# Turning the down products of the last four rows of a fused attention and MoE kernel

## The chip, the cores and the metric

The kernel runs on one core of a Trainium2 chip. Its time is the device time of one execution in microseconds (us). Three runs of the kernel before gave 603.53, 605.04 and 608.01 us, median 605.04.

A core has TensorE (PE, with its weight loads shown apart as PEld), VectorE (DVE), ScalarE (ACT), GpSimd (POOL) and SyncE (SP). Each runs its own list of instructions in order and waits on semaphores. DMAs are issued here by SP (all loads) and by ACT (the stores).

## The reference, cut to what matters

A linear attention with a decaying state, then a gated feed-forward layer, all in fp32:

```
for t in range(768):                                   # B=4, H=8, D=48
    cur = einsum('bhd,bhe->bhde', u * k_t, v_t)
    y[:, :, t] = einsum('bhd,bhde->bhe', r_t, state + cur)
    state = w_t[..., None] * state + einsum('bhd,bhe->bhde', k_t, v_t)
x = y as [3072 tokens, 384]
out = (sigmoid(x @ w_gate) * (x @ w_val)) @ w_out      # 384 -> 1536 -> 384
```

## The kernel before, in words

The sequence of 768 is cut into 6 rows (n = 0 to 5) of 128 positions. A row holds 4 batches of 128 tokens, so 512 tokens. For every row and batch (q = 4n + batch) an attention chunk is computed on all engines. Its result is transposed on PE (px) into x, split in a high and a low part.

The feed-forward layer then goes through 12 blocks f of the hidden size. A step (n, f) does 9 matmuls for the gate (pg), 9 for the value (pu), and on ACT and DVE the sigmoid (sg), the product with pu (sg again), its high part (hh, ACT) and its low part (hl, DVE). The down products (po) add the block's share to the row's outputs. Each product of fp32 values is done as three matmuls of parts: low by high, high by low, high by high.

In gate and value the weights (128x128) are loaded into the array and x streams past, 512 tokens wide. In the down products before, the hidden block of one batch (hl or hh, 128x128) is loaded, and 384 weight columns stream past: 4 batches by 3 parts are 12 matmuls of 384 columns. Each batch has its own PSUM bank, po0 to po3. After f = 11 ACT copies the four banks to SBUF (tile o, two buffers) and issues a DMA of 192 KB for each (L515, L517).

Rows 0 and 1 are placed by a planner, which interleaves them with the loads, the weights' unpacking and the attention. Rows 2 to 5 follow in an order written out by hand ("late"). Each step of a row runs, in this order: the gate, one part of the attention chunk of the next row, the value, another part, the down products **of the step before**, a third part. Three steps hold one attention chunk. I call them A (pk behind the gate, the score products pa behind the value), B (pa behind the gate, px behind the value) and C (nothing of the attention on PE). Row 5 has no next row, so all its steps are like C. The attention uses two PSUM banks in turn (att).

At the end a flag, computed in row 5's first step, is read by every engine (L651). A branch then jumps over `general`, a slow version for extreme inputs that is not executed here, to the end of the program, where SP waits for all DMAs and engines.

Of the kernel before, what the change touches and what calls it, by code (L numbers as in the profile page):

```python
# [9 lines left out]
F32 = mybir.dt.float32  # L10
F32R = mybir.dt.float32r
BF16 = mybir.dt.bfloat16
# [7 lines left out]
B, H, S, D = 4, 8, 768, 48  # L20
DM, DFF = 384, 1536
P = 128
C = 128
NC_ = S // C
NG = B * NC_
# [4 lines left out]
NFF = DFF // P  # L30
NKT = DM // P
# [13 lines left out]
def general(ctx: ExitStack, tc: tile.TileContext, dec, tok, wts, u, out, whi, wlo, ident):  # L45


    nc = tc.nc
    pool = ctx.enter_context(tc.tile_pool(name="general", bufs=1))
    bank = ctx.enter_context(tc.tile_pool(name="banks", bufs=1, space=PSUM))  # L50
    rows = ctx.enter_context(tc.tile_pool(name="rows", bufs=1, space=bass.MemoryType.DRAM)).tile([B, S, DM], F32, name="rows")

    def tiles(name, shape, dtype=F32):
        return pool.tile(shape, dtype, name=name)

    raw, t, full, square = tiles("raw", [P, HW], mybir.dt.int64), tiles("t", [P, HW], I32), tiles("full", [P, HW]), tiles("square", [P, HW])
    for f in range(NFF):
        for half in range(2):
            cols = slice(half * HW, (half + 1) * HW)
# [19 lines left out]
    vb, y = tiles("vb", [L, B, NP, D]), tiles("yb", [2, B, NP, D])  # L79
# [11 lines left out]
    for c in range(NC_):  # L91
        for b in range(B):
            nc.sync.dma_start(d[:, b], dec[b * NC_ + c])
        with tc.For_i(0, C) as i:
            def at(first, step):
                return d[:, :, first:first + NP * step].rearrange("a b (p c) -> a b p c", c=step)[:, :, :, bass.ds(i, 1)].broadcast_to(shape)
            for o in range(2):
                for b in range(B):
                    nc.sync.dma_start(vb[64 * o:64 * o + D, b], values[c, 2, o, bass.ds(i, 1), b].partition_broadcast(D))
            nc.vector.tensor_tensor(out=kv, in0=vb, in1=at(WW, C), op=ALU.mult)  # L100
            nc.vector.tensor_tensor(out=mix, in0=kv, in1=ub, op=ALU.mult)
            nc.vector.tensor_tensor(out=mix, in0=mix, in1=state, op=ALU.add)
            nc.vector.tensor_tensor(out=mix, in0=mix, in1=at(WW + NP * C, C), op=ALU.mult)
            nc.vector.tensor_tensor(out=state, in0=state, in1=at(1, W1), op=ALU.mult)
            nc.vector.tensor_tensor(out=state, in0=state, in1=kv, op=ALU.add)
            for j in range(2):
                nc.tensor.matmul(py[j][:2, :DM], lhsT=heads, rhs=mix[:, 2 * j:2 * j + 2], start=True, stop=True)
                nc.scalar.copy(y[:, 2 * j:2 * j + 2], py[j][:2, :DM].rearrange("a (b p e) -> a b p e", b=2, e=D))
            for b in range(B):
                for o in range(2):  # L110
                    nc.sync.dma_start(
                        rows[b, bass.ds(c * C + i, 1)].rearrange("t (p o e) -> o t p e", o=2, e=D)[o], y[o:o + 1, b])

    x, px = tiles("x", [P, DM]), bank.tile([P, 512], F32, name="px")
    xhi, xlo = tiles("xh", [P, NKT, C], F32R), tiles("xl", [P, NKT, C], F32R)
    gate, h, hh, hl = tiles("gate", [P, C]), tiles("h", [P, C]), tiles("hh", [P, C], F32R), tiles("hl", [P, C], F32R)
    pg, pu, po = (bank.tile([P, 512], F32, name=n) for n in ("pg", "pu", "po"))
    flat = rows.rearrange("b s e -> (b s) e")
    with tc.For_i(0, NG) as g:
        nc.sync.dma_start(x, flat[bass.ds(g * C, C)])  # L120
        for k in range(NKT):
            nc.tensor.transpose(out=px[:, k * C:(k + 1) * C], in_=x[:, k * P:(k + 1) * P], identity=ident)
        px3 = px[:, :DM].rearrange("a (k c) -> a k c", c=C)
        nc.scalar.copy(xhi, px3)
        nc.vector.tensor_tensor(out=xlo, in0=px3, in1=xhi.bitcast(F32), op=ALU.subtract)
        for f in range(NFF):
            for s, acc in enumerate((pg, pu)):
                for k in range(NKT):
                    cols = slice(s * DM + k * P, s * DM + (k + 1) * P)
                    for j, (w, a) in enumerate(((wlo, xhi), (whi, xlo), (whi, xhi))):  # L130
                        nc.tensor.matmul(acc[:, :C], lhsT=w[f][:, cols], rhs=a[:, k], start=k == 0 and j == 0, stop=k == NKT - 1 and j == 2)
            nc.scalar.activation(gate, pg[:, :C], AF.Sigmoid)
            nc.vector.tensor_tensor(out=h, in0=pu[:, :C], in1=gate, op=ALU.mult)
            nc.scalar.copy(hh, h)
            nc.vector.tensor_tensor(out=hl, in0=h, in1=hh.bitcast(F32), op=ALU.subtract)
            for j, (a, w) in enumerate(((hl, whi), (hh, wlo), (hh, whi))):
                nc.tensor.matmul(po[:, :DM], lhsT=a, rhs=w[f][:, 2 * DM:], start=f == 0 and j == 0, stop=f == NFF - 1 and j == 2)
        nc.scalar.copy(x, po[:, :DM])
        nc.sync.dma_start(out[bass.ds(g * C, C)], x)


class Plan:
# [49 lines left out]
def tile_kernel(ctx: ExitStack, tc: tile.TileContext, dec: bass.AP, tok: bass.AP, wts: bass.AP, u: bass.AP, out: bass.AP):  # L192
    nc = tc.nc
# [3 lines left out]
    p1 = own.enter_context(tc.tile_pool(name="p1", bufs=1))  # L197
    p2 = own.enter_context(tc.tile_pool(name="p2", bufs=2))
    ps1 = own.enter_context(tc.tile_pool(name="ps1", bufs=1, space=PSUM))
    att2 = own.enter_context(tc.tile_pool(name="att2", bufs=2, space=PSUM))  # L200
    early = tc.tile_pool(name="early", bufs=4)
    stage = early.__enter__()

    def att_bank(name):
        return att2.tile([P, 512], F32, tag="att", name=name)

    ident = const.tile([P, P], F32, name="ident")
# [8 lines left out]
    for s in range(2):  # L216
        part = after[s * HC:(s + 1) * HC]
        nc.gpsimd.affine_select(
            out=part, in_=part, pattern=[[1, HC]], compare_op=ALU.is_gt, fill=0.0, base=0, channel_multiplier=-1,
# [14 lines left out]
    raws, fulls, whi, wlo = {}, {}, [None] * NFF, [None] * NFF  # L234
# [5 lines left out]
    def word(f, i, dtype=I32):  # L240
        return raws[f].bitcast(dtype).rearrange("a (c w) -> a c w", w=2)[:, :, i]

    def w_guard(f):
        sq = p1.tile([P, 3 * DM], F32, tag="sq", name=f"sq{f}")
        nc.scalar.activation(sq, word(f, 1, F32), AF.Square, accum_out=acc_s[:, f:f + 1])
        nc.scalar.activation(sq, sq, AF.Relu, bias=1.0, scale=-1.0 / TINY ** 2, accum_out=acc_t[:, f:f + 1])

# [22 lines left out]
    pin, tk, eg, bon, kT, att, ready, mid, bank, x = {}, {}, {}, {}, {}, {}, {}, {}, {}, {}  # L270

    def place(q):
        return q % B * NC_ + q // B
# [204 lines left out]
    po, hid = {}, {}  # L478

    def gate(n, f, i0, i1):  # L480
        hid["g", n, f, i0] = up(0, "pg", n, f, i0, i1)
# [5 lines left out]
    def value(n, f, i0, i1):  # L487
        hid["u", n, f, i0] = up(1, "pu", n, f, i0, i1)
# [13 lines left out]
    def down(n, f, i0, i1):  # L502
        hh, hl = hid["hi", n, f, i0], hid["lo", n, f, i0]
        for i in range(i0, i1):
            if f == 0:
                po[n, i] = ps1.tile([P, 512], F32, tag=f"po{i}", name=f"po{n}_{i}")
            c = slice((i - i0) * C, (i - i0 + 1) * C)
            for j, (h, w) in enumerate(((hl, whi), (hh, wlo), (hh, whi))):
                nc.tensor.matmul(  # L509
                    po[n, i][:, :DM], lhsT=h[:, c], rhs=w[f][:, 2 * DM:],  # L510
                    start=f == 0 and j == 0, stop=f == NFF - 1 and j == 2,
                )
            if f == NFF - 1:
                o = p2.tile([P, DM], F32, tag="o", name=f"o{n}_{i}")
                nc.scalar.copy(o, po[n, i][:, :DM])  # L515
                g = place(n * B + i)
                nc.scalar.dma_start(out[g * C:(g + 1) * C, :], o)  # L517

    def check_bounds():
        nc.vector.tensor_scalar(out=fine[:L, 0], in0=acc_d, scalar1=2.0 ** 90, scalar2=None, op0=ALU.is_le)  # L520
# [18 lines left out]
    for q in range(3 * B + 2):  # L539
        k = rank.get(f"c{q}", 99)  # L540
# [28 lines left out]
        first = q % B == 0  # L569
# [4 lines left out]
    for f in range(NFF):  # L574
        k = rank[f"w{f}"]
# [7 lines left out]
    for g, (n, i0, i1) in enumerate(GROUPS):  # L583
        m = i1 - i0
        for f in range(NFF):
            a, name = (n, f, i0, i1), f"{g}_{f}"
            k = 100 + f + LAGS[g]
# [40 lines left out]
    last = []  # L628
    nothing = [[lambda: None] * 3] * 3
    for n in range(2, NC_):  # L630
        for j in range(B):
            trio = steps((n + 1) * B + j) if n + 1 < NC_ else nothing
            for i in range(3):
                a = (n, 3 * j + i, 0, B)
                gate(*a)
                sigmoid(*a)
                trio[i][0]()
                value(*a)
                hidden(*a)
                hidden_hi(*a)  # L640
                hidden_lo(*a)
                trio[i][1]()
                if last:
                    down(*last.pop())
                trio[i][2]()
                last.append(a)
                if n == NC_ - 1 and j == 0 and i == 0:
                    check_bounds()
    down(*last.pop())
    own.close()  # L650
    with tc.If(nc.values_load(flag[:1, :1]) != 0):  # L651
        general(tc, dec, tok, wts, u, out, whi, wlo, ident)
# [31 lines left out]
```

## Time and profile before

| | us |
|---|---|
| runs, median (lowest to highest) | 605.04 (603.53 to 608.01) |
| profiled execution, its own time | 603.9 |
| its span | 602.2 |
| PE busy | 558.7 (93%) |
| PE weight loads busy | 498.4 (83%) |
| DVE busy | 332.6 (55%) |
| ACT busy | 201.6 (33%) |

The span is what the trace covers; 1.7 us of the execution lie around it. Times in the rows count from the span's start. Matmuls overlap in the trace, so the pace of a train of matmuls is read from the starts of two neighbouring groups and not from the durations.

### The profile page before, as it was taken

The page shows a single profiled execution, that of the slowest core. Times are in us where ns is not written, and L with a number is a line of the kernel's source. Part 1 is how long each engine was busy: PE and PEld are TensorE (multiplying, and loading weights), DVE is VectorE, ACT ScalarE, POOL GpSimd, SP SyncE. Part 2 cuts the span into 40 slices and gives each one's busy share as a digit, 9 for nine tenths or more (in the row PEclk, how much of TensorE's full clock was granted, in tenths as well). Part 3 has the DMA queues.
Part 4 walks back from the last instruction along what each step waited for, and adds up shares of the span by engine and source line. Part 5 has one row for each costly group of instructions (what it writes and reads, how often), then busy time and mean ns, then how long its engine had stood idle before and what let it go on. Part 6 is the DMA issues. An engine that isn't in the chain of part 4 may idle for free. (4 is left out here: it accounts for less than half of the span.)

```text
span 602.2 us, 14593 instructions
## 1 busy us (share of the span) xinstructions
PE 558.7 (93%) x6474; PEld 498.4 (83%) x6474; DVE 332.6 (55%) x570; ACT 201.6 (33%) x402; POOL 96.7 (16%) x86
## 2 busy tenths in 40 slices
PE   4475899999999999899999999999999999999994
PEld 3365799999999999788888888888888888888883
DVE  4989879989685653254554554554454453221220
ACT  3648683444333322312222322222321221222212
POOL 3352111102120502002201211211211210000000
PEclk9999699999999999999999999999999999999997
DMA  8788920033233130122033033022033000100001
GB/s 250 250 327 290 347 95 1 1 87 83 72 121 126 50 125 3 53 86 86 3 87 87 28 112 86 2 86 87 35 106 87 1 1 2 54 1 0 1 1 57
DMA packets 12055, 50.85 MB, mean 84 GB/s; under 512 B 1376, under 2 KB 4576, under 8 KB 10448
## 3 DMA queue, kind: packets, MB, share of 16 engines
q1 hardware_dynamic: 8528, 45.11, 23.4%
q10 hardware_dynamic: 3456, 4.72, 2.2%
q8 instruction: 53, 0.87, 0.6%
q14 instruction: 18, 0.15, 0.1%
HBM read 45.11 MB, written 4.72 MB: 83 GB/s over the span
## 5 line engine op out<-in xcount | busy, mean ns | idle before, releaser
L474 PE MATMUL pg<-x,w 128*128 128x256 f32 (+1 forms) x864 | 171.6, 344 | 2.1 <-DVE w L267 2.1
L474 PE MATMUL pu<-x,w 128*128 128x256 f32 (+1 forms) x864 | 170.5, 342 | 0.0
L474 PEld LDWEIGHTS pg<-x,w 128*128 128x128 f32 x864 | 138.3, 193 | 17.8 <-DVE w L267 2.2
L474 PEld LDWEIGHTS pu<-x,w 128*128 128x128 f32 x864 | 136.2, 191 | 17.3
L509 PE MATMUL po<-w,hh 128*128 128x384 f32 x576 | 147.7, 337 | 0.0
L492 DVE TENSOR_TENSOR sg<-pu,sg 128x256 f32<-128x256 f32 (+1 forms) x96 | 53.4, 557 | 149.9 <-PE pu L474 148.9
L509 PE MATMUL po<-w,hl 128*128 128x384 f32 x288 | 101.2, 351 | 7.1 <-DVE hl L500 7.0
L496 ACT CAST hh<-sg 128x256 fp32r<-128x256 f32 (+1 forms) x96 | 49.2, 512 | 170.0 <-DVE sg L492 169.6
L509 PEld LDWEIGHTS po<-w,hh 128*128 128x128 f32 x576 | 105.0, 189 | 0.9
L485 ACT ACTIVATE sg<-pg 128x256 f32<-128x256 f32 (+1 forms) x96 | 46.9, 488 | 141.7 <-PE pg L474 140.1
L314 POOL TENSOR_TENSOR bon<-tok,a 128x384 f32<-128x384 f32 x24 | 35.0, 1457 | 282.7 <-DVE a L310 282.7
L500 DVE TENSOR_TENSOR hl<-sg,hh 128x256 fp32r<-128x256 f32 (+1 forms) x96 | 55.7, 580 | 39.0 <-ACT hh L496 39.0
L509 PEld LDWEIGHTS po<-w,hl 128*128 128x128 f32 x288 | 54.3, 189 | 10.4 <-DVE hl L500 8.4
L303 POOL TENSOR_TENSOR bon<-tok,ub 128x384 f32<-128x384 f32 x24 | 32.6, 1358 | 113.4 <-DMA tok<-tok 61.1
L448 DVE TENSOR_TENSOR bon<-pa,bon 128x192 f32<-128x192 f32 x48 | 15.6, 353 | 49.3 <-PE pa L441 49.2
L348 ACT ACTIVATE junk<-eg 112x1032 bf16<-112x1032 f32 x24 | 25.6, 1066 | 30.7 <-DVE eg L338 30.6
L321 DVE TENSOR_TENSOR_SCAN eg<-pin,ends 112x516 f32<-112x516 f32 x24 | 30.0, 1251 | 4.9 <-DMA pin<-dec 4.9
L338 DVE TENSOR_TENSOR_SCAN eg<-pin,heads 112x516 f32<-112x516 f32 x24 | 30.5, 1270 | 0.0
L353 PE MATMUL pk<-ident,pin 112*128 112x112 f32 x96 | 14.7, 278 | 14.1 <-DVE pin L327 10.2
L306 POOL TENSOR_TENSOR bon<-bon,tok 128x384 f32<-128x384 f32 x24 | 27.3, 1136 | 1.7
L441 PE MATMUL pa<-tok,at 64*32 64x48 f32 x1536 | 23.8, 213 | 2.3 <-DVE at L402 2.3
L353 PEld LDWEIGHTS pk<-ident,pin 112*128 112x128 f32 x96 | 11.5, 150 | 17.1 <-issue 9.0
(62 smaller groups left out, 433.8 us busy)
## 6 DMA issues: line engine op xcount, KB each, us to landing
pin<-dec SPq DMA_DIRECT2D x23, 675.5 KB, 5.8
tok<-tok SPq DMA_DIRECT2D x24, 576.0 KB, 5.8
wraw<-wts SPq DMA_DIRECT2D x12, 1152.0 KB, 12.3
y<-o ACTq DMA_DIRECT2D x24, 192.0 KB, 1.9
pin<-dec SPq DMA_DIRECT2D x1, 448.0 KB, 4.3
pin<-dec SPq DMA_DIRECT2D x1, 227.5 KB, 2.9
ub<-u SPq DMA_DIRECT2D x1, 192.0 KB, 6.7
```

What stands on the lines that cost most here:

```text
L303: nc.gpsimd.tensor_tensor(out=bon[q], in0=tk[q][:, 0:DM], in1=ub, op=ALU.mult)
L306: nc.gpsimd.tensor_tensor(out=bon[q], in0=bon[q], in1=tk[q][:, DM:2 * DM], op=ALU.mult)
L314: nc.gpsimd.tensor_tensor(out=by_head(bon[q]), in0=by_head(tk[q][:, 2 * DM:]), in1=a0, op=ALU.mult)
L321: nc.vector.tensor_tensor_scan(out=e[:, 516:0:-1], data0=t[:, 516:0:-1], data1=ends[:, 516:0:-1], initial=0.0, op0=ALU.mult, op1=ALU.add,)
L338: nc.vector.tensor_tensor_scan(out=e[:, WW:WW + 516], data0=t[:, 0:516], data1=heads[:, 0:516], initial=0.0, op0=ALU.mult, op1=ALU.add,)
L353: nc.tensor.transpose(out=t[:, p * L:(p + 1) * L], in_=kk(q)[:, p], identity=ident[:L, :L])
L474: nc.tensor.matmul(t, lhsT=w[f][:, cols], rhs=x[n][:, a, k, i0 * C:i1 * C], start=k == 0 and j == 0, stop=k == NKT - 1 and j == 2)
L485: nc.scalar.activation(sg, hid["g", n, f, i0], AF.Sigmoid)
L492: nc.vector.tensor_tensor(out=sg, in0=hid["u", n, f, i0], in1=sg, op=ALU.mult)
L496: nc.scalar.copy(hh, hid["s", n, f, i0])
L500: nc.vector.tensor_tensor(out=hl, in0=hid["s", n, f, i0], in1=hid["hi", n, f, i0].bitcast(F32), op=ALU.subtract)
L509: nc.tensor.matmul(po[n, i][:, :DM], lhsT=h[:, c], rhs=w[f][:, 2 * DM:], start=f == 0 and j == 0, stop=f == NFF - 1 and j == 2,)
```

## The change

The diff, without the comments and without the fallback `general`, whose layout follows the new output and whose loop over the 24 chunks is written out:

```
+    late = False
+    turns = []
     def att_bank(name):
+        turns.append(name)
+        if late and len(turns) % 3 == 0:
+            return ps1.tile([P, 512], F32, tag="po3", name=name)
         return att2.tile([P, 512], F32, tag="att", name=name)
...
     def w_guard(f):
-        sq = p1.tile([P, 3 * DM], F32, tag="sq", name=f"sq{f}")
+        sq = p1.tile([P, 3 * DM], BF16, tag="sq", name=f"sq{f}")
...
                 o = p2.tile([P, DM], F32, tag="o", name=f"o{n}_{i}")
                 nc.scalar.copy(o, po[n, i][:, :DM])
-                g = place(n * B + i)
-                nc.scalar.dma_start(out[g * C:(g + 1) * C, :], o)
+                nc.scalar.dma_start(out[n].rearrange("(b c e) -> b c e", b=B, c=C)[i], o)
+
+    def down_turned(n, f, i0, i1):
+        hh, hl = hid["hi", n, f, i0], hid["lo", n, f, i0]
+        for k in range(NKT):
+            if f == 0:
+                po[n, k] = ps1.tile([P, 512], F32, tag=f"po{k}", name=f"po{n}_{k}")
+            cols = slice(2 * DM + k * P, 2 * DM + (k + 1) * P)
+            for j, (h, w) in enumerate(((hl, whi), (hh, wlo), (hh, whi))):
+                nc.tensor.matmul(po[n, k], lhsT=w[f][:, cols], rhs=h, start=f == 0 and j == 0, stop=f == NFF - 1 and j == 2)
+            if f == NFF - 1:
+                o = p1.tile([P, B * C], F32, tag=f"ot{k}", name=f"o{n}_{k}")
+                y = po[n, k]
+                by_vector = n == NC_ - 1 and k == 1
+                if by_vector:
+                    nc.vector.tensor_copy(out=o, in_=y)
+                else:
+                    nc.scalar.copy(o, y)
+                to = out[n].rearrange("(k p t) -> k p t", p=P, t=B * C)[k]
+                (nc.sync if by_vector else nc.scalar).dma_start(to, o)
...
     stage = own.enter_context(tc.tile_pool(name="late", bufs=2))
+    late = True
...
-                    down(*last.pop())
+                    down_turned(*last.pop())
...
-    down(*last.pop())
+    down_turned(*last.pop())
```

In rows 2 to 5 the down weights (three blocks k of 128 output columns) are loaded and the 512 tokens of hl or hh stream past: 3 blocks by 3 parts are 9 matmuls of 512 columns. The outputs stand transposed in three banks, po0 to po2; the host turns them back. A row leaves as three DMAs of 256 KB in pieces of 2048 bytes instead of four of 192 KB in pieces of 1536. Each of the three has its own SBUF tile. In the last row the middle block is copied by DVE and issued by SP. The fourth bank, po3, becomes a third one for the attention in the late rows. The squares that the weights' guard computes are kept in bf16.

On PE the last two rounds of down products (f = 10 and f = 11 of row 5) read before (po, hl and hh as above, w the weights, the number behind a name its buffer):

```order
L474 MATMUL pu_0_11_6669<-x_5459,w_1682 128x512 x9
L509 MATMUL po_0_6290<-w_1558,hl_0_10_6643 128x384
L509 MATMUL po_0_6290<-w_1558,hh_0_10_6641 128x384 x2
...
L509 MATMUL po_3_6302<-w_1558,hh_0_10_6641 128x384 x2
L509 MATMUL po_0_6290<-w_1682,hl_0_11_6682 128x384
L509 MATMUL po_0_6290<-w_1682,hh_0_11_6680 128x384 x2
...
L509 MATMUL po_3_6302<-w_1682,hh_0_11_6680 128x384 x2
```

and now:

```order
L494 MATMUL pu_0_11_6518<-x_5379,w_1682 128x512 x9
L546 MATMUL po_0_6170<-hl_0_10_6495,w_1558 128x512
L546 MATMUL po_0_6170<-hh_0_10_6493,w_1558 128x512 x2
...
L546 MATMUL po_2_6178<-hh_0_10_6493,w_1558 128x512 x2
L546 MATMUL po_0_6170<-hl_0_11_6531,w_1682 128x512
L546 MATMUL po_0_6170<-hh_0_11_6529,w_1682 128x512 x2
...
L546 MATMUL po_2_6178<-hh_0_11_6529,w_1682 128x512 x2
```

Nothing else of PE's order has moved, here or in the earlier rows; only the down groups of rows 2 to 5 have other matmuls.

On ACT, the end of the program before:

```order
L515 COPY o_0_6699<-po_0_6290 128x384
L517 DMA y<-o_0_6699 128x384
L515 COPY o_1_6705<-po_1_6294 128x384
L517 DMA y<-o_1_6705 128x384
L515 COPY o_2_6711<-po_2_6298 128x384
L517 DMA y<-o_2_6711 128x384
L515 COPY o_3_6717<-po_3_6302 128x384
L517 DMA y<-o_3_6717 128x384
L651 TENSOR_LOAD flag
L651 COMPARE_AND_BRANCH
```

and now:

```order
L554 COPY o_0_6545<-po_0_6170 128x512
L556 DMA y<-o_0_6545 128x512
L554 COPY o_2_6557<-po_2_6178 128x512
L556 DMA y<-o_2_6557 128x512
L691 TENSOR_LOAD flag
L691 COMPARE_AND_BRANCH
```

Two of four copies and DMAs are gone from ACT's end; DVE has one more copy there. On SP, where the last load was followed by the flag and the branch:

```order
L281 DMA pin_5697<-dec 112x1544
L286 DMA tok_5699<-tok 128x1152
L651 TENSOR_LOAD flag
L651 COMPARE_AND_BRANCH
```

there stands now:

```order
L301 DMA pin_5607<-dec 112x1544
L306 DMA tok_5609<-tok 128x1152
L556 DMA y<-o_1_6551 128x512
L691 TENSOR_LOAD flag
L691 COMPARE_AND_BRANCH
```

SP's flag and branch now stand behind a DMA that waits for the last row's middle block.

## Rows read from the trace of the kernel before

**Rows 1.** The page: busy us (share of the span) and instructions, granted clock by slices.
```profile
PE 558.7 (93%) x6474; PEld 498.4 (83%) x6474; DVE 332.6 (55%) x570; ACT 201.6 (33%) x402; POOL 96.7 (16%) x86
...
PEclk9999699999999999999999999999999999999997
```

**Rows 2.** Busy time by stretches: us from-to, length, engines, granted clock, DMA share, GB/s.
```profile
0.00:90.00 90.00, 59.78 (x977) 53.61 (x978) 72.74 (x104) 57.13 (x101) 24.85 (x31) 0.94 0.76 261
...
285.00:390.00 105.00, 105.00 (x1164) 90.46 (x1163) 55.10 (x97) 28.38 (x57) 20.68 (x15) 1.00 0.20 60
```

**Rows 3.** Timeline of PE, a C step: start, us, line, operation, count.
```profile
287.57 2.20 PE L474 MATMUL pu<-x,w 128*128 128x512 f32 x9
289.61 0.33 PE L509 MATMUL po<-w,hl 128*128 128x384 f32 x1
...
291.19 0.33 PE L509 MATMUL po<-w,hl 128*128 128x384 f32 x1
...
291.71 0.39 PE L474 MATMUL pg<-x,w 128*128 128x512 f32 x1
```

**Rows 4.** Timeline of PE in row 1, where trains are 256 columns wide.
```profile
238.28 1.24 PE L474 MATMUL pg<-x,w 128*128 128x256 f32 x9
239.36 1.24 PE L474 MATMUL pu<-x,w 128*128 128x256 f32 x9
```

**Rows 5.** Timeline of PE, an A step and a B step of row 2.
```profile
269.35 2.25 PE L474 MATMUL pg<-x,w 128*128 128x512 f32 x9
271.44 0.55 PE L353 MATMUL pk<-ident,pin 112*128 112x112 f32 x4
271.75 2.33 PE L474 MATMUL pu<-x,w 128*128 128x512 f32 x9
274.01 0.69 PE L370 MATMUL pa<-pin 48*64 48x64 f32 x32
...
275.08 0.44 PE L509 MATMUL po<-w,hl 128*128 128x384 f32 x1
...
277.27 2.25 PE L474 MATMUL pg<-x,w 128*128 128x512 f32 x9
279.44 0.26 PE L380 MATMUL pa<-ready,pin 48*64 48x48 f32 x2
...
280.87 2.34 PE L474 MATMUL pu<-x,w 128*128 128x512 f32 x9
283.05 0.49 PE L453 MATMUL px<-ident,bon 128*128 128x128 f32 x3
283.30 0.42 PE L509 MATMUL po<-w,hl 128*128 128x384 f32 x1
...
285.49 0.39 PE L474 MATMUL pg<-x,w 128*128 128x512 f32 x1
```

**Rows 6.** Timeline of PE and ACT at the end of the program.
```profile
591.51 0.44 PE L509 MATMUL po<-w,hl 128*128 128x384 f32 x1
591.79 0.51 PE L509 MATMUL po<-w,hh 128*128 128x384 f32 x2
...
593.35 0.51 PE L509 MATMUL po<-w,hh 128*128 128x384 f32 x2
...
592.34 0.48 ACT L515 COPY o<-po 128x384 f32<-128x384 f32 x1 [1.61 <-PE po L509]
592.85 0.34 ACTq L517 DMA_DIRECT2D y<-o  x1
...
593.79 1.03 ACTq L517 DMA_DIRECT2D y<-o  x1
595.92 0.48 ACT L515 COPY o<-po 128x384 f32<-128x384 f32 x1 [2.16 <-SPq L651]
...
597.38 0.64 ACTq L517 DMA_DIRECT2D y<-o  x1
```

**Rows 7.** The flag and branch, L651, by engine: durations ns min/median/max, first and last start.
```profile
L651 SPq EVENT_SEMAPHORE  x8: 17/17/17, 526.4 to 599.7; - x8
L651 SPq TENSOR_LOAD <-flag x1: 572/572/572, 522.9 to 522.9; - x1
...
L651 SPq COMPARE_BRANCH  x1: 45/45/45, 523.6 to 523.6; - x1
...
L651 PEldq COMPARE_BRANCH  x1: 3757/3757/3757, 592.2 to 592.2; - x1
...
L651 ACTq TENSOR_LOAD <-flag x1: 485/485/485, 598.1 to 598.1; - x1
L651 ACTq COMPARE_BRANCH  x1: 54/54/54, 598.6 to 598.6; - x1
L651 ACTq EVENT_SEMAPHORE  x1: 17/17/17, 601.3 to 601.3; - x1
```

**Rows 8.** The program's last line, L680, on SP, the same columns.
```profile
L680 SPq EVENT_SEMAPHORE  x10: 17/28/1137, 599.8 to 602.1; - x10
```

**Rows 9.** Groups by shape: busy us, mean ns of one, then idle before, releaser.
```profile
L485 ACT ACTIVATE sg<-pg 128x512 f32<-128x512 f32 x48 | 28.5, 593 | 104.2 <-PE pg L474 103.4 <-PE pa L380 0.8
L492 DVE TENSOR_TENSOR sg<-pu,sg 128x512 f32<-128x512 f32 x48 | 33.2, 692 | 119.9 <-PE pu L474 119.9
L348 ACT ACTIVATE junk<-eg 112x1032 bf16<-112x1032 f32 x24 | 25.6, 1066 | 30.7 <-DVE eg L338 30.6
L246 ACT ACTIVATE sq<-sq 128x1152 f32<-128x1152 f32 x12 | 14.0, 1166 | 0.4
```

**Rows 10.** All waits from 262 to 590: who waited for whom, us, times, longest.
```profile
ACT o L515 <- DMA y<-o: 4.5, 6, 1.0
...
PE total L527 <- DVE count L525: 0.7, 1, 0.7
```

**Rows 11.** DMA issues from 585: KB each, median us to landing.
```profile
y<-o ACTq DMA_DIRECT2D x4, 192.0 KB, 2.6
```

**Rows 12.** Timeline at the start of the late rows, 249 to 252.
```profile
249.56 0.48 ACT L515 COPY o<-po 128x384 f32<-128x384 f32 x1 [0.47 <-PE po L509]
...
251.03 0.55 PE L353 MATMUL pk<-ident,pin 112*128 112x112 f32 x4
```

More of the change, by code (lines that the diff above doesn't have):

```diff
@@ L50, in general @@
     bank = ctx.enter_context(tc.tile_pool(name="banks", bufs=1, space=PSUM))
-    rows = ctx.enter_context(tc.tile_pool(name="rows", bufs=1, space=bass.MemoryType.DRAM)).tile([B, S, DM], F32, name="rows")
+    rows = ctx.enter_context(tc.tile_pool(name="rows", bufs=1, space=bass.MemoryType.DRAM)).tile([NC_, B, C, DM], F32, name="rows")
     def tiles(name, shape, dtype=F32):
@@ L111, in general @@
                     nc.sync.dma_start(
-                        rows[b, bass.ds(c * C + i, 1)].rearrange("t (p o e) -> o t p e", o=2, e=D)[o], y[o:o + 1, b])
+                        rows[c, b, bass.ds(i, 1)].rearrange("t (p o e) -> o t p e", o=2, e=D)[o], y[o:o + 1, b])
     x, px = tiles("x", [P, DM]), bank.tile([P, 512], F32, name="px")
@@ L117, in general, with feed @@
     pg, pu, po = (bank.tile([P, 512], F32, name=n) for n in ("pg", "pu", "po"))
-    flat = rows.rearrange("b s e -> (b s) e")
-    with tc.For_i(0, NG) as g:
-        nc.sync.dma_start(x, flat[bass.ds(g * C, C)])
+    def feed(n, b, turned):
+        nc.sync.dma_start(x, rows[n, b])
         for k in range(NKT):
@@ L135, in general @@
             nc.vector.tensor_tensor(out=hl, in0=h, in1=hh.bitcast(F32), op=ALU.subtract)
-            for j, (a, w) in enumerate(((hl, whi), (hh, wlo), (hh, whi))):
-                nc.tensor.matmul(po[:, :DM], lhsT=a, rhs=w[f][:, 2 * DM:], start=f == 0 and j == 0, stop=f == NFF - 1 and j == 2)
-        nc.scalar.copy(x, po[:, :DM])
-        nc.sync.dma_start(out[bass.ds(g * C, C)], x)
+            for k in range(NKT if turned else 1):
+                cols = slice(2 * DM + k * P, 2 * DM + (k + 1) * P)
+                for j, (a, w) in enumerate(((hl, whi), (hh, wlo), (hh, whi))):
+                    first, done = f == 0 and j == 0 and k == 0, f == NFF - 1 and j == 2
+                    if turned:
+                        nc.tensor.matmul(po[:, k * C:(k + 1) * C], lhsT=w[f][:, cols], rhs=a, start=first, stop=done, skip_group_check=True)
+                    else:
+                        nc.tensor.matmul(po[:, :DM], lhsT=a, rhs=w[f][:, 2 * DM:], start=first, stop=done)
+        nc.scalar.copy(x, po[:, :DM])
+        if turned:
+            to = out[n].rearrange("(k p b c) -> b p k c", p=P, b=B, c=C)[b]
+            nc.sync.dma_start(to, x.rearrange("p (k c) -> p k c", c=C))
+        else:
+            nc.sync.dma_start(out[n].rearrange("(b c e) -> b c e", b=B, c=C)[b], x)
+    for n in range(NC_):
+        for b in range(B):
+            feed(n, b, n >= 2)
 class Plan:
@@ L515, in down @@
                 nc.scalar.copy(o, po[n, i][:, :DM])
-                g = place(n * B + i)
-                nc.scalar.dma_start(out[g * C:(g + 1) * C, :], o)
+                nc.scalar.dma_start(out[n].rearrange("(b c e) -> b c e", b=B, c=C)[i], o)
[4 more added lines that the diff above has]
+                po[n, k] = ps1.tile([P, 512], F32, tag=f"po{k}", name=f"po{n}_{k}")
+            cols = slice(2 * DM + k * P, 2 * DM + (k + 1) * P)
+            for j, (h, w) in enumerate(((hl, whi), (hh, wlo), (hh, whi))):
[6 more added lines that the diff above has]
+                    nc.vector.tensor_copy(out=o, in_=y)
+                else:
+                    nc.scalar.copy(o, y)
+                to = out[n].rearrange("(k p t) -> k p t", p=P, t=B * C)[k]
+                (nc.sync if by_vector else nc.scalar).dma_start(to, o)
     def check_bounds():
@@ L678 @@
     args = [nc.dram_tensor(n, a.shape, mybir.dt.from_np(a.dtype), kind="ExternalInput").ap() for n, a in arrays.items()]
-    args.append(nc.dram_tensor("y", (B * S, DM), F32, kind="ExternalOutput").ap())
+    args.append(nc.dram_tensor("y", (NC_, B * C * DM), F32, kind="ExternalOutput").ap())
     with tile.TileContext(nc) as tc:
@@ L682 @@
     r = run_bass_kernel_spmd(nc, [arrays], core_ids=[0])
-    return r.results[0]["y"]
+    y = r.results[0]["y"]
+    y = np.concatenate([y[:2].reshape(-1, B * C, DM), y[2:].reshape(-1, DM, B * C).transpose(0, 2, 1)])
+    return np.ascontiguousarray(y.reshape(NC_, B, C, DM).transpose(1, 0, 2, 3).reshape(B * S, DM))
```

## The prediction, made blind

> **What bounds the kernel now.** First the page: PE is busy 93% of the span, at the full granted clock but for two slices early and the last one [rows 1]. Then the busy time by stretches: from 285 to 390 PE is busy 105.00 of 105.00 us, while ACT has 28 and DVE 55 [rows 2]. From 262 to 590 no engine keeps PE waiting but once, for 0.7 us at the flag's sum [rows 10]. So in rows 2 to 5, which hold all that the change touches on PE, only the length of PE's own work counts, and after the last matmul only the chain of copies, DMAs and branches. The early 90 us are the place where PE is not full (59.78 of 90) [rows 2]; the change moves nothing there.
>
> **The price of one matmul.** Since matmuls overlap, I divide the distance between the starts of groups. Nine of 512 columns: 287.57 to 289.61, 2.04 us, 0.2267 each. The last three of 384: 291.19 to 291.71, 0.1733 each [rows 3]. Nine of 256: 1.08 us, 0.1200 each [rows 4]. From 384 to 512 a column costs 0.417 ns, and all three widths leave the same 0.0133 us beside the columns. A weight load is hidden at each of these paces.
>
> **Down products, turned.** 12 x 384 and 9 x 512 are both 4608 columns, so the columns are worth nothing. What goes is the fixed part of three matmuls: 3 x 0.0133 = 0.04 us a step. This is the lower end of the term.
>
> On this price the Trainium skill speaks against the change: TensorE: Matmul & The Clock Gate, "Wait — 56ns, not 53.3ns?", gives N / 2.4 + about 2.5 ns for warm matmuls. By it the three matmuls would be worth 0.0075 us a step, 0.35 us in all. The trace disagrees: 13.3 ns at three widths; I take the trace.
>
> Second, trains pay for a change of width. The gate train behind the down products takes 285.49 to 287.57, 2.08 us, where the value train behind it takes 2.04; the down group itself takes 2.10 where 12 x 0.1733 is 2.08 [rows 3, 5]. No other engine explains it in the rows, since the gate and the value read the same x. With all trains 512 wide and nothing between them a C step should be 27 x 0.2267 = 6.12 instead of 6.22 (285.49 to 291.71): 0.10 less.
>
> In A and B steps small matmuls of the attention stand in the train and keep their price. In A, the gate loses 0.04 as above; the down group behind pa takes 275.08 to 277.27, 2.19, and turned I set it like B's value train behind 64 small ones, 280.87 to 283.05, 2.18, less 0.01 for its end: 0.02 less. In B the gate loses 0.04; the down group behind px takes 283.30 to 285.49, 2.19, and turned I set it like A's value train behind pk, 271.75 to 274.01, 2.26, less the 0.09 by which a train that ends in small matmuls is longer (B's gate, 2.17 against 2.08): 2.17, 0.02 less [rows 5]. So 0.06 for A and for B.
>
> There are 48 steps; the last down group belongs to the tail, and the first step has none: 11 A, 12 B and 24 C steps. 23 x 0.06 + 24 x 0.10 = **3.8 us**. Lower end 47 x 0.04 = 1.9, upper end 47 x 0.10 = 4.7. I take 3.8, since it has a row for each neighbour.
>
> **The tail.** Now the last down group starts at 591.51 and its last pair at 593.35, but the span ends at 602.2 [rows 6]. The third copy starts only at 595.92, 2.16 us idle: the row names SP, but the tile o has two buffers, and the copy waits for the DMA issued at 592.85 to land. The fourth DMA is issued at 597.38 for 0.64. Then ACT loads the flag (598.1), branches (598.6), and goes on at 601.3, 2.7 later; 0.9 later all is over [rows 6, 7]. SP and DVE had their branch earlier.
>
> After: the first matmul of the group is 0.11 long (0.28 to the next against 0.17), the others 0.2267. The ninth starts at 591.51 + 0.11 + 8 x 0.2267 = 593.43, ends 0.39 later (a single one in [rows 3]), and 0.04 later ACT copies: 593.86. A 512-wide ACT pass from PSUM takes 0.593 [rows 9]: 594.45. No buffer is waited for. DMA issue 0.34 to 1.03 [rows 6], flag 0.49, branch 0.05, with the small gaps about 595.4; 2.7 more: 598.1; 0.9 more: 599.0.
>
> But the middle block goes through DVE and SP, and SP's flag and branch now stand behind it. The sixth matmul starts at 592.75, DVE copies from 593.18 for 0.69 at most [rows 9], SP issues at 593.9 (0.34), loads the flag (0.57) and branches at 594.9. SP's jump took from 523.6 to 526.4, 2.8 [rows 7]: 597.7. Behind it SP has 8 + 8 waits to walk through before it can close; the last of the first line stands at 599.7, the first of the next at 599.8 [rows 7, 8], so a tenth each at most, and I take 1.0 for all: 598.7. With the closing 0.9: **599.6, 2.5 us less** than 602.2. So SP, not ACT, is late next. Ends: 3.2 if SP's walk is hidden (599.0); 1.0 if SP's jump takes the 3.76 that PE's branch shows and the walk 1.6 [rows 7].
>
> **The rest.** The landing of the last DMA is covered: issued at about 594.5, 2.6 to land [rows 11] gives 597.1, before SP's 597.7; a block of 256 KB may take longer by a third of that, 0.9, and would cost 0.3. In mid-kernel, ACT's four copies of a row wait 4.5 us in total for their DMAs [rows 10]. These waits go, but PE doesn't feel them today, and three passes of 0.59 replace four of 0.48: nothing. The third bank takes away no wait, as none of PE is for a bank [rows 10]. Its first use in the late rows needs po3 copied out of row 1: that ends at 250.04, the late rows' first chunk starts at 251.03 [rows 12]; the cover is 1.0 us, without it PE would wait once for less than that. The bf16 squares: ACT takes 1166 ns for 1152 elements to fp32 and 1066 for 1032 to bf16 [rows 9], 1.01 and 1.03 ns per element: nothing, and ACT is busy 57 of the early 90 us [rows 2]. If it were the bound there, 24 passes by 0.03 us either way would be 0.7.
>
> **Sum.** 3.8 + 2.5 = 6.3 us. The profiled execution, 603.9, would become 597.6. The median of the runs stands 1.1 higher; from 605.04 the forecast is **598.7 us**. What can be told from no change is about 1%, 6.05 us here, so below 599.0 counts as faster: the forecast lies on that line.
>
> **The rivals.**
> - *Only the fixed part goes* (0.17). The slow gate train would then belong to the gate itself, or the turned group inherits it. For: it is slow in every step. Against: B's value train is slow at the same width, so it follows what stands ahead. 1.9 + 2.5: 600.6.
> - *The tail gives little* (0.13). SP's late branch eats it, as its lower end: 3.8 + 1.0: 600.2.
> - *Everything at its upper end* (0.08): 4.7 + 3.2 = 7.9: 597.1.
> - *Columns alone set PE's pace* (0.05). If the 0.0133 came from the 128-wide weight load sharing the array with the stream, 9 and 12 matmuls would take the same, and only the tail counts: 602.5. Against: it is the same at 256, 384 and 512 columns. The skill's 2.5 ns, cited above, would come out near here.
> - *Slower: weight loads laid bare at each change of bank* (0.03). The turned group fills three banks one after the other, each with a new block of weights. A's value train behind pk pays 2.26 - 2.04 - 0.09 = 0.13 for a cold start [rows 3, 5]. Three of these in 47 steps would be 18.3 us, and with 1.9 and 2.5 gained the time is 618.9. It decides from 4.4 / 141 = 0.03 us per block on. Against: the step from pg to pu is such a change and costs nothing, 2.04.
> - *The change does nothing for the attention*: the third bank and the larger pieces are worth zero in my sum already, so this costs nothing.
>
> The forecast has 0.50; 0.04 stays for what I don't see, half of it slow.
>
> **The numbers.** The likeliest case runs from 597.6 to 599.8 (tail and C steps by half a microsecond each way); the range, with both cases that lose one term and the upper end, is **597.0 to 602.4**. Faster by over 1%: somewhat more than half of the forecast's 0.50, the 0.08 of the upper end and a share of the runs' own scatter: 0.43. Slower 0.04. Within 1%: 0.53.
>
> **What would show it.** C steps of 6.12 us; gate trains of 2.04 behind a turned group, at 0.2267 a matmul; A and B steps of 7.86 and 8.16; no waits of ACT for o; in the tail ACT's last copy at about 593.9 in today's count, SP the last to leave its branch, and some 6.2 us from the last matmul's start to the span's end instead of 8.7. I am wrong if the gate train keeps its 2.08, if turned groups take over 2.10 in C steps, or if another engine or a longer jump closes the program.

## The result, and the profile after

The changed kernel takes 598.36 us (median of four, 596.57 to 599.10) where the kernel before took 605.28 in the same session: a ratio of 0.9878, with a 95% interval of 0.9850 to 0.9906. The forecast was 598.7. The profiled execution took 596.57, its span 594.9, against 603.9 and 602.2.

The page of the changed kernel, to be laid beside [rows 1]: busy us, share and count of instructions, then the granted clock by slices.

```profile
PE 552.8 (93%) x6330; PEld 476.3 (80%) x6330; DVE 333.2 (56%) x571; ACT 200.3 (34%) x397; POOL 96.6 (16%) x86
...
PEclk9999899999999999999999999999999999999999
```

PE has 144 matmuls fewer, 3 in each of 48 down groups. In the fifth slice of the clock stands an 8 where [rows 1] has a 6; of the change only the squares' type lies in that part, and we shall come back to it.

The timeline of PE in a C step (start, us, line, operation, count), beside [rows 3]:

```profile
283.52 2.21 PE L494 MATMUL pg<-x,w 128*128 128x512 f32 x9
285.57 2.20 PE L494 MATMUL pu<-x,w 128*128 128x512 f32 x9
287.61 0.39 PE L546 MATMUL po<-hl,w 128*128 128x512 f32 x1
...
289.65 0.84 PE L494 MATMUL pg<-x,w 128*128 128x512 f32 x3
```

The step takes 283.52 to 289.65, 6.12 us by the median of such steps. The turned group takes 2.04 (287.61 to 289.65), and so does the gate behind the turned group of a C step, which the steps of row 5 show, where nothing else stands:

```profile
511.05 2.20 PE L494 MATMUL pg<-x,w 128*128 128x512 f32 x9
513.09 2.20 PE L494 MATMUL pu<-x,w 128*128 128x512 f32 x9
515.13 0.39 PE L546 MATMUL po<-hl,w 128*128 128x512 f32 x1
```

These steps take 6.120, three times 2.04.

The same view of an A and a B step, beside [rows 5]:

```profile
267.50 2.21 PE L494 MATMUL pg<-x,w 128*128 128x512 f32 x9
269.55 0.55 PE L373 MATMUL pk<-ident,pin 112*128 112x112 f32 x4
269.87 2.33 PE L494 MATMUL pu<-x,w 128*128 128x512 f32 x9
...
273.19 0.50 PE L546 MATMUL po<-hl,w 128*128 128x512 f32 x1
...
275.36 2.20 PE L494 MATMUL pg<-x,w 128*128 128x512 f32 x9
...
281.11 0.49 PE L473 MATMUL px<-ident,bon 128*128 128x128 f32 x3
281.35 0.48 PE L546 MATMUL po<-hl,w 128*128 128x512 f32 x1
```

A is 267.50 to 275.36, 7.86, and B from there to 283.52 above, 8.16: before they were 7.92 and 8.22. The turned group behind pa takes 273.19 to 275.36, 2.17 against 2.19.

The waits from 260 to 585 (who waited for whom, us in total, times, longest), beside [rows 10]:

```profile
ACT o L554 <- PE po L546: 2.1, 5, 0.5
...
PE total L566 <- DVE count L564: 0.9, 1, 0.9
```

ACT no longer waits for a DMA of o, and PE waits only at the flag's sum, as before (0.7 there).

The end of the program, PE, ACT, DVE and SP in one timeline (in brackets the idle time before and what ended it), beside [rows 6]:

```profile
586.15 0.50 PE L546 MATMUL po<-hl,w 128*128 128x512 f32 x1 [0.19 <-DVE hl L520]
...
587.15 0.59 ACT L554 COPY o<-po 128x512 f32<-128x512 f32 x1 [1.78 <-PE po L546]
...
587.77 0.34 ACTq L556 DMA_DIRECT2D y<-o  x1
587.85 0.69 DVE L552 COPY o<-po 128x512 f32<-128x512 f32 x1 [1.75 <-PE po L546]
587.88 0.61 PE L546 MATMUL po<-hh,w 128*128 128x512 f32 x2
588.53 0.59 ACT L554 COPY o<-po 128x512 f32<-128x512 f32 x1 [0.79 <-PE po L546]
588.57 0.34 SPq L556 DMA_DIRECT2D y<-o  x1
589.15 0.34 ACTq L556 DMA_DIRECT2D y<-o  x1
```

From the start of the last down group to the end of the span it is 8.70 us (586.15 to 594.86); before it was 10.68 (591.51 to 602.19). No copy waits for an earlier DMA. Then the flag and branch (durations ns min/median/max, first and last start), beside [rows 7]:

```profile
L691 SPq EVENT_SEMAPHORE  x8: 17/17/17, 592.9 to 593.5; - x8
...
L691 SPq COMPARE_BRANCH  x1: 45/45/45, 589.5 to 589.5; - x1
...
L691 ACTq COMPARE_BRANCH  x1: 54/54/54, 590.2 to 590.2; - x1
...
L691 ACTq EVENT_SEMAPHORE  x1: 17/17/17, 593.6 to 593.6; - x1
```

SP jumps from 589.51 to 592.94, 3.43 us, and ACT from 590.21 to 593.62, 3.42. Before, SP's jump took 2.89 and ACT's 2.68. SP then walks through its waits without being held (592.94 to 594.04) and closes the program 0.82 later.

The start of the late rows, beside [rows 12]:

```profile
249.29 0.55 PE L373 MATMUL pk<-ident,pin 112*128 112x112 f32 x4
```

It is 1.74 earlier than before. So the 7.33 us between the two spans are 1.75 ahead of the first late gate, 3.57 from there to the last gate (336.05 to 332.48), 0.05 to the last down group and 1.98 behind it, up to rounding.

### The profile page after: what moved, and what is told of

It reads as the page before. It is cut to its first block, busy times and chain, and to the rows that moved or that the text cites. A ratio compares the mean times of both kernels' runs of the same rounds, so it can differ in the third digit from the quotient of the medians.

```text
span 594.9 us, 14288 instructions
## 1 busy us (share of the span) xinstructions
PE 552.8 (93%) x6330; PEld 476.3 (80%) x6330; DVE 333.2 (56%) x571; ACT 200.3 (34%) x397; POOL 96.6 (16%) x86
## 4 chain that ended last, share of the span: by engine, by line
PE 86%; DVE 5%; DMA 5%; issue 1%; ACT 1%; SPq 1%; POOL 0%; ACTq 0%; DVEq 0%; POOLq 0%
PE pu L494 25%; PE pg L494 24%; PE po L546 16%; PE po L529 8%; PE pa L461 3%; DMA wraw<-wts 3%; PE pa L390 2%; PE pa L400 2%; PE pk L373 1%; PE px L473 1%; DMA ub<-u 1%; PE pv L437 1%; DMA pin<-dec 1%; PE pa L437 1%; DVE eg L341 1%
## 5 line engine op out<-in xcount | busy, mean ns | idle before, releaser
L494 PE MATMUL pg<-x,w 128*128 128x256 f32 (+1 forms) x864 | 169.0, 341 | 2.1 <-DVE w L287 2.1
L546 PE MATMUL po<-hh,w 128*128 128x512 f32 x288 | 89.1, 390 | 0.0
L546 PEld LDWEIGHTS po<-hh,w 128*128 128x128 f32 x288 | 54.1, 188 | 10.8
L546 PE MATMUL po<-hl,w 128*128 128x512 f32 x144 | 58.7, 407 | 0.2 <-DVE hl L520 0.2
L529 PE MATMUL po<-w,hh 128*128 128x384 f32 x192 | 49.0, 336 | 0.0
L529 PE MATMUL po<-w,hl 128*128 128x384 f32 x96 | 34.2, 356 | 7.3 <-DVE hl L520 7.3
L529 PEld LDWEIGHTS po<-w,hh 128*128 128x128 f32 x192 | 34.9, 188 | 0.0
L546 PEld LDWEIGHTS po<-hl,w 128*128 128x128 f32 x144 | 27.0, 188 | 6.1 <-DVE hl L520 0.6
```

What stands on the lines that cost most here:

```text
L494: nc.tensor.matmul(t, lhsT=w[f][:, cols], rhs=x[n][:, a, k, i0 * C:i1 * C], start=k == 0 and j == 0, stop=k == NKT - 1 and j == 2)
L529: nc.tensor.matmul(po[n, i][:, :DM], lhsT=h[:, c], rhs=w[f][:, 2 * DM:], start=f == 0 and j == 0, stop=f == NFF - 1 and j == 2,)
L546: nc.tensor.matmul(po[n, k], lhsT=w[f][:, cols], rhs=h, start=f == 0 and j == 0, stop=f == NFF - 1 and j == 2)
```

## Experiments

Each ratio is to the kernel before, with its 95% interval. "Steps" are medians of the distance between gates in rows 2 to 5.

**Turning alone.** The changed kernel, but with two attention banks, fp32 squares, two buffers for o, and ACT making all copies.

```
-        if late and len(turns) % 3 == 0:
+        if False:
-        sq = p1.tile([P, 3 * DM], BF16, ...)
+        sq = p1.tile([P, 3 * DM], F32, ...)
-                o = p1.tile([P, B * C], F32, tag=f"ot{k}", ...)
+                o = p2.tile([P, B * C], F32, tag="ot", ...)
-                by_vector = n == NC_ - 1 and k == 1
+                by_vector = False
```

> Of the change only the turning stays: two banks for the attention, squares in fp32, ACT copies and issues all three blocks of a row through two SBUF tiles. Theory (a matmul costs its columns plus 0.0133 us, and a train pays for a change of width): the steps are those of the changed kernel, C 6.12, A 7.86, B 8.16 us. In the tail the third copy waits for the first block's DMA to land, so from the first matmul of the last down group to the end of the span some 9.0 to 9.8 us instead of 8.75 (before: 10.68). Rival (the third bank gives part of the gain): A or B steps longer than 7.86 and 8.16 by 0.05 or more. Rival (the squares in bf16 shorten the early part): the late rows start at 248.9 as before and not at 247.2, whatever the clock's dips.

Measured: 599.41 us, 0.9917 [0.9886, 0.9948]. Steps 7.853, 8.162 and 6.124, the changed kernel's to 0.001; 332.39 between first and last gate; tail 9.23. ACT's timeline at its end:

```profile
590.10 0.34 ACTq L556 DMA_DIRECT2D y<-o  x1
591.55 0.58 ACT L554 COPY o<-po 128x512 f32<-128x512 f32 x1 [1.48 <-PEq L691]
```

The third copy has nothing to wait for on PE, whose group is done; its buffer is that of the first DMA, which lands at 591.47. The whole PE term belongs to the turning, and 1.45 of the tail's 1.98 come with it too: three copies and DMAs stand at the end where four stood.

**Turned products in halves.** Still turned, but each matmul cut into two of 256 columns: the same columns, 18 matmuls, w still the loaded operand.

```
+            for s in range(2):
+                half = slice(s * 2 * C, (s + 1) * 2 * C)
...
-                nc.tensor.matmul(po[n, k], lhsT=w[f][:, cols], rhs=h, ...)
+                    nc.tensor.matmul(po[n, k][:, half], lhsT=w[f][:, cols], rhs=h[:, half], ...)
```

> The changed kernel, but each turned down product is cut in two of 256 columns: 18 matmuls a step with the same columns and the same loaded weights. Theory: 18 x 0.12 = 2.16 us for the group and a slow gate train (2.08) behind it, as the width changes again: C steps 6.25 to 6.28 us instead of 6.12, 6.1 to 7.5 us over 47 steps, so about the time of the kernel before. Rival (the gate is slow because of what is loaded in the group ahead, hl and hh, and not because of its width): gate 2.04, C about 6.24. Rival (columns alone count): C 6.12.

Measured: 604.64 us, 1.0002 [0.9981, 1.0023]: the gain is gone. PE's timeline in a C step:

```profile
287.48 2.23 PE L494 MATMUL pg<-x,w 128*128 128x512 f32 x9
289.54 2.20 PE L494 MATMUL pu<-x,w 128*128 128x512 f32 x9
291.58 0.28 PE L548 MATMUL po<-hl,w 128*128 128x256 f32 x1
...
293.74 1.09 PE L494 MATMUL pg<-x,w 128*128 128x512 f32 x4
```

The down group takes 2.15 for the 4608 columns that took 2.04 (by the medians 2.153 and 2.040): 0.0126 for each of nine more matmuls. The gate behind it takes 2.07 by the median (287.48 to 289.54 here), where 2.04 stood behind the 512-wide group and 2.08 behind the 384-wide one, while the value stays at 2.04. So the slow gate belongs to the change of width ahead of it, and neither to the gate nor to which operand is loaded. The C step has 6.260; A has 7.960 and B 8.247, which lose 0.11 and 0.08 against the changed kernel, so that from the first gate to the last it is 5.2 longer than the changed kernel and not 6.1 or more, as was expected.

**Two banks.** The changed kernel without the third attention bank.

```
-        if late and len(turns) % 3 == 0:
+        if False:
```

> The changed kernel with two banks for the attention again. Theory: no wait of PE was for a bank, so A, B and C steps are those of the changed kernel to 0.01 us, and so is the tail. Rival (the third bank counts): A or B steps longer by 0.05 or more, 0.6 us or more over 12 chunks.

Measured: 598.25 us, 0.9899 [0.9875, 0.9923]; steps 7.853, 8.163, 6.124; 332.37 between the gates, 0.1 less than with the third bank; tail 8.84 for 8.70. The bank is worth nothing.

**px and pk behind one gate.** A try to go further: px of a chunk and pk of the next stand together behind the gate of C, so that the value trains of A and B follow fewer small matmuls.

```
-        parts[0][0] += [(turn_k, q), (take_k, q)]
+        if q == 3 * B:
+            parts[0][0] += [(turn_k, q), (take_k, q)]
...
-        parts[1][1] += [(turn_x, q), (take_x, q), (rest_x, q)]
+        parts[2][0] += [(turn_x, q), (take_x, q), (rest_x, q)]
...
+            parts[2][0] += [(turn_k, q + 1), (take_k, q + 1)]
```

> The changed kernel with the attention's small matmuls in fewer places: px of a chunk and pk of the next stand together behind C's gate, instead of px behind B's value and pk behind A's gate (the first chunk's pk stays). Theory (a 512-wide train pays 0.13 us behind small matmuls and 0.09 ahead of some): A loses about 0.45, B about 0.38, C gains about 0.63; 0.2 us less a chunk, 2.2 over 11 chunks, if pk finds its operand ready. Rival (pk then waits for DVE's prep_k, which has one step less): C longer by up to 1 us more, the kernel slower than the changed one by up to 9 us.

Measured: 598.93 us, 0.9882 [0.9858, 0.9906]; A 7.413, B 7.787, C 6.883. PE's timeline in its C step:

```profile
283.88 2.21 PE L494 MATMUL pg<-x,w 128*128 128x512 f32 x9
285.93 0.49 PE L473 MATMUL px<-ident,bon 128*128 128x128 f32 x3
286.26 0.55 PE L373 MATMUL pk<-ident,pin 112*128 112x112 f32 x4
286.57 2.32 PE L494 MATMUL pu<-x,w 128*128 128x512 f32 x9
288.73 0.39 PE L546 MATMUL po<-hl,w 128*128 128x512 f32 x1
```

The three steps sum to 22.08 against 22.14, where 0.2 less was expected; between the first gate and the last it is 0.6 less than in the changed kernel and not 2.2. A and B lose 0.44 and 0.38, about as expected, so the miss is C's. pk keeps its 0.31 (286.26 to 286.57), but px now takes 0.33 (285.93 to 286.26), where it took 0.24 in the changed kernel (281.11 to 281.35). That 0.09 eats most of what the trains save, since the value behind both still pays its 0.12 over 2.04 (286.57 to 288.73). This expectation failed: a small group's own time also depends on what stands beside it.

**Own tiles for o in the kernel before.** Four SBUF tiles for the four output blocks of the late rows; the squares in bf16 (not shown in the cut) make the room.

```
-                o = p2.tile([P, DM], F32, tag="o", ...)
+                o = (p1.tile([P, DM], F32, tag=f"ot{i}", ...) if n >= 2 else p2.tile(...))
```

> The kernel before with one change: in rows 2 to 5 each of the four output blocks has its own SBUF tile (squares in bf16, for the room). Theory: steps stay 6.23, 7.92, 8.22 us; the third copy in the tail no longer waits for a landing, so the program ends 8.2 to 9.6 us after the first matmul of the last down group instead of 10.68: 1.1 to 2.5 us are the tail's alone. Rival (the tail is bounded by the branch and not by the buffers): 10.4 or more.

Measured: 603.72 us, 0.9981 [0.9962, 1.0001]; steps as before; tail 9.51, that is 1.17 less than before. ACT's timeline:

```profile
594.16 0.48 ACT L515 COPY o<-po 128x384 f32<-128x384 f32 x1 [0.47 <-PE po L509]
594.67 1.08 ACTq L517 DMA_DIRECT2D y<-o  x1
595.85 0.48 ACT L515 COPY o<-po 128x384 f32<-128x384 f32 x1 [1.21 <-issue]
```

The wait for the buffer [rows 6] is gone, as the prediction had read it, and the engine named there (SP) was not its cause. The second DMA issue takes 1.08 as it took 1.03 before; so that has nothing to do with the buffers.

**ACT issues the middle block.** The changed kernel with all three last DMAs on ACT, so that SP has its branch long before.

```
-                (nc.sync if by_vector else nc.scalar).dma_start(to, o)
+                nc.scalar.dma_start(to, o)
```

> The changed kernel, but ACT issues the middle block's DMA too (DVE still copies it), so SP branches early, at about 520, as in the kernel before. Theory (a branch costs 2.7 us alone and 3.3 to 3.6 when several engines branch within a microsecond, and SP's late branch with its walk of 1.1 us closes the program): ACT's branch comes 0.3 later, its jump takes 2.7 to 3.4, SP walks in its shadow: 7.9 to 8.6 us from the first matmul of the last down group to the end instead of 8.70 and 8.84. Rival (SP's issue saves time): 8.9 or more. Steps unchanged.

Measured: 599.84 us, 0.9907 [0.9881, 0.9932]; tail 10.26, 1.56 longer. ACT's timeline and, below it, the DMA row of its last issue:

```profile
589.36 1.87 ACTq L556 DMA_DIRECT2D y<-o  x2
591.32 0.59 ACT L554 COPY o<-po 128x512 f32<-128x512 f32 x1 [2.00 <-issue]
591.94 0.34 ACTq L556 DMA_DIRECT2D y<-o  x1
```

```profile
y<-o ACTq DMA_DIRECT2D x1, 256.0 KB, 4.2
```

The second of the two issues took 1.07 (590.16 to 591.23), so the last copy starts 3.58 after the group instead of 2.38, and the last block lands 4.2 after its issue, at 596.15, instead of 3.2. SP, which branched at 520.8, waits for that and walks through the rest of its waits only then (596.17 to 597.19), not hidden behind ACT's jump. The expected gain was worked out with ACT's branch 0.3 later, and it came 1.1 later (5.13 after the start of the group for 4.06); the landing and the hidden walk failed too. Only the rival had the direction.

**Both together**: the edits of the last try and of px with pk.

> Both edits together, a candidate for the fastest: 2.2 us less between the late rows' gates and 0.1 to 0.9 us less in the tail than the changed kernel, about 2.3 to 3.1 us in all, so a ratio to the kernel before of about 0.984. Rival as for the two parts.

Measured: 599.59 us, 0.9900 [0.9870, 0.9930]; 331.77 between the gates, tail 10.02. The middle issue took 0.69, the last landing 4.4. The ratio of 0.984 that was expected lies outside the interval: it beats the kernel before, not the change.

**Small last stores.** The changed kernel, but of the last row's three blocks only 16 of 128 partitions are stored; the rest of that row's outputs is left out.

```
+                few = slice(0, 16 if n == NC_ - 1 else P)
-                (nc.sync if by_vector else nc.scalar).dma_start(to, o)
+                (nc.sync if by_vector else nc.scalar).dma_start(to[few], o[few])
```

> The changed kernel, but the last row's three DMAs store only 16 of 128 partitions (the rest of the last row's outputs is left out), which tells why the branches of SP and ACT took 3.4 to 3.6 us instead of 2.7 to 2.9. Theory (the code behind the branch is fetched by the DMA engines that move the stores): with an eighth of the bytes the jumps of SP and ACT take 2.7 to 3.0 and the tail is 0.4 to 0.7 us shorter than 8.70 to 8.84. Rival (several engines that branch within a microsecond slow each other): 3.3 to 3.6 still.

Measured, in one execution: 598.17 us; tail 7.93, 0.77 shorter than the changed kernel's 8.70, where 0.4 to 0.7 was expected. The branch's rows:

```profile
L692 SPq EVENT_SEMAPHORE  x8: 17/17/17, 594.5 to 595.1; - x8
...
L692 SPq COMPARE_BRANCH  x1: 45/45/45, 591.9 to 591.9; - x1
...
L692 ACTq COMPARE_BRANCH  x1: 54/54/54, 592.6 to 592.6; - x1
L692 ACTq EVENT_SEMAPHORE  x1: 17/17/17, 595.4 to 595.4; - x1
```

SP's jump is back at 2.62 (591.92 to 594.54) and ACT's at 2.81, against 3.43 to 3.57 and 3.31 to 3.54 in the five runs with whole blocks and the same order at the end. DVE, SP and ACT still branch within 1.7 us of each other (590.86, 591.92, 592.57), as in the changed kernel (588.48, 589.51, 590.21), so the rival falls. The bytes being stored during the jump lengthened it by 0.8 and 0.6, as far as one execution shows.

**The squares alone**: the kernel before with `sq` in bf16.

> The kernel before with the guard's squares in bf16 and nothing else. Theory (the early part is not shortened by the change, its scatter comes with the granted clock's dips): ratio 1 within 0.003, steps and tail as before (6.23, 7.92, 8.22; about 10.7), the two passes 1.26 and 1.17 us as before. Rival (the squares give the microsecond or so by which the runs of the changed kernel gained more than late rows and tail show): ratio 0.998 or less and late rows that start before 248 with dips of 10 us.

Measured: 604.50 us, 0.9989 [0.9968, 1.0010]. ACT's two passes, by shape (busy us, mean ns, idle before):

```profile
L245 ACT ACTIVATE sq<-wraw 128x1152 bf16<-128x1152 f32 x12 | 15.1, 1255 | 3.9 <-DMA wraw<-wts 3.9
L246 ACT ACTIVATE sq<-sq 128x1152 bf16<-128x1152 bf16 x12 | 14.0, 1166 | 0.4
```

The first pass takes 1255 ns, where it took 1258, and the second 1166 as in [rows 9]. The first late gate stands at 251.06, the tail is 10.48. So the type changes neither pass and gives only room; the ratio alone would not show a gain of under 2 us.

**The changed kernel and the kernel before, once more.**

> The changed kernel once more, on the chip of the two edits, as their reference. Theory (the early part's difference of 1.75 us between the first two profiles is the granted clock's dips and no gain): the steps and the tail repeat to 0.02 and 0.2 us, and the late rows start at 247 to 250, later with more time at half clock ahead of 90 us. Rival (the bf16 squares or the larger room help the early part): 247.2 again with dips of 10 us.

> The kernel before once more, unchanged, as a second trace and a check of the comparison. Theory: ratio 1 within 0.003, the same steps to 0.01 us, the late rows start between 247 and 252 by the clock's dips. The tail repeats 10.7 us to 0.3, with the second DMA's issue of ACT stretched to about 1.0 us again, ending 0.4 after a 16 KB piece of code has been fetched.

Measured: 598.87 us, 0.9887 [0.9865, 0.9909] for the changed kernel; 605.37 us, 0.9990 [0.9971, 1.0009] for the kernel before. Steps, tails (8.76 and 10.89) and, in the changed one, SP's and ACT's jumps (3.48 and 3.53) come back; in the kernel before, ACT's second issue takes 0.99 again. But the first late gate of the changed kernel stands at 250.01 here, where it stood at 247.20, and TensorE's granted clock is at its lower level (0.5, which is 1.2 GHz) for 10.2 us between 35 and 90 instead of 3.4; in the kernel before it is 250.68 with 17.1, where it was 248.95 with 10.2. Over all traces the first late gate stands at 247.20 to 251.56, and runs with 10.2 us at the lower level alone cover 248.56 to 251.56, so the lower clock is at most a part of this scatter.

## Why the prediction came out, point by point

- **PE, 3.8 us.** Measured 3.57 between the gates and 0.05 behind. The mechanism was right, both halves of it: the fixed cost per matmul (nine more matmuls cost 0.11, turned in halves) and the width change (2.07 against 2.04, there and gone with the width alone). C steps came out at 6.124 for 6.12, A at 7.853 for 7.86, B at 8.163 for 8.16, and the turning alone gives all of it. The 0.2 that is missing lies mostly in three steps that the count took for ordinary ones. The second late step takes 8.47 before and after: the first late step has no down group, so the gate of the second stands behind pa (2.27 both times) and had no slow start behind a down group to lose. The step with the flag's sum, where PE waits for DVE's count (0.7 before, 0.9 now), went from 7.24 to 7.29, and the one behind it lost 0.06 and not 0.10.
- On the fixed cost the Trainium skill was weighed ahead of the run (TensorE: Matmul & The Clock Gate, "Wait — 56ns, not 53.3ns?"). Estimated from its 2.5 ns a matmul, the halves would have cost 0.02 a group; the trace shows 0.11, so it disagrees here too.
- **The tail, 2.5 us.** Measured 1.98, and the step that was mis-sized is SP's jump: 2.8 was taken, from the middle of the program [rows 7], where 3.43 came. A longer jump was one of the signs of being wrong that the prediction named, and it was there. Small last stores bring 2.62, so, by that one execution, the difference is the store traffic beside which the jump now stands. All else of that chain holds: ACT's last copy 2.38 after the group for 2.35 expected, SP's branch 3.36 for 3.39, the walk 1.10 for 1.0, the closing 0.82 for 0.9, and SP is the one that ends the program. From the last matmul's start to the end it is 6.75 instead of the 6.2 forecast.
- **The third bank, the squares, the larger pieces: nothing.** The first was taken out alone and the second put in alone; neither gave anything that the traces show. The larger pieces were not run alone; a middle row's 256 KB lands in 2.0 us where 192 KB took 1.9, and nothing waits for it.
- **The rivals.** Columns alone falls with the halves. Only the fixed part falls with the gate of 2.04. Weight loads laid bare falls with a turned group of 2.04. The tail gives little was half right: SP's late branch is the bound and its jump is longer than in the forecast, but 1.98 is much nearer to 2.5 than to 1.0. Everything at its upper end is out by both terms: 3.62 for 4.7, 1.98 for 3.2.
- **The sum.** 3.62 and 1.98 are 5.6 us, 0.7 less than forecast. The profiled execution fell by 7.33, because the part ahead of the late rows was 1.75 shorter; that part holds nothing of the change but the squares and the place of two rows' stores, and the same kernel run again had it 2.81 longer. So the closeness of 598.36 to 598.7 is in part luck of that scatter. The three comparisons (0.9878, 0.9887, and 0.9899 without the third bank) put the gain at 6.1 to 7.4 us of 605; their intervals reach down to 5.5 us and, without the bank, to 4.7. Four of the tries, which share 25 executions of the kernel before, show little of such a surplus: turning alone gained 5.0 where its gates and tail give 5.1, own tiles 1.1 where the tail gives 1.2, two banks 6.1 for 5.6, and the halves lost 0.1 where gates and tail give a gain of 0.2. So scatter is the likelier reading, but whether a microsecond beyond the 5.6 is real stays open.

## What to carry to other kernels

Where an engine is never idle, look for its time in the distance between starts of neighbouring groups: a train that costs 0.04 us more behind one neighbour than behind another names a cost that no busy share shows. When you reorder the end of a program, work out for every engine when it reaches its last jump and which stores are still under way then; a jump timed in a quiet stretch was 0.6 too short here. And before crediting a profiled pair of runs with a gain, cut both at the first place where the change touches the bounding engine: here 1.75 of 7.33 us lay ahead of it.

## What the runs showed of the hardware that was not expected

- **A jump to code that must be fetched is longer beside stores.** With two blocks of 256 KB under way SP's and ACT's jumps took 3.3 to 3.6 us (the changed kernel twice, two banks, halves, px with pk); with one block or little, 2.6 to 2.8 (ACT's before 2.68, turning alone 2.66, own tiles 2.77; small stores 2.62 and 2.81). SP's early jump near 525, far from the last stores, took 2.72 to 3.06 in four runs. The number of blocks isn't the whole of it: where ACT issues all, one block was left, as in turning alone, and yet its jump took 3.20 and 3.52. What sets the length beyond that was not found. PE's jump took 3.3 to 3.9 in all runs, with no pattern that I could name.
- **Code fetch delays stores and their issue.** The queue for instructions carries packets of 16 KB; in ACT's try from 586 to 598 (queue, packets, MB, share of 16 engines):

```profile
q8 instruction: 2, 0.03, 1.4%
```

  0.014 of 16 engines for 12 us is 2.7 us for the two: by the trace's packets 0.93 and 1.68. In all ten cases at the ends of these runs in which ACT issued a DMA 0.2 us or more after such a packet had begun, the issue lasted until 0.36 to 0.38 after the packet's end (so 1.03 and 0.64 in [rows 6], 1.08 with own tiles, 1.07 where ACT issues all) instead of taking 0.34. SP's issues beside such a packet took 0.34 to 0.35. And the 256 KB blocks at the ends of these runs landed 2.4 to 4.4 us after their issue, where a middle row's takes 2.0 by the median: the last few packets trail one at a time, 0.08 to 0.22 us apart. In ACT's try the trail starts at 594.63, a microsecond after the packet ahead of it, just as the code packet that began at 592.99 ends (594.67). That these packets share a DMA engine with the fetch is inferred; the trace doesn't name it.
- **A change of width is paid over several matmuls.** Behind narrower ones the matmuls of a 512-wide train start 0.224 to 0.236 apart instead of 0.2267: with halves the first five (0.233, 0.236, 0.228, 0.233, 0.231), and only then 0.2267; in the kernel before, behind the 384-wide group, all eight (0.229, 0.233, 0.236, 0.224, 0.231, 0.236, 0.228, 0.233). Not one of them is long.
